# Two zero fills moved behind the last gather, weights one slot forward, and the last gate's small work moved to POOL

## The chip, the cores and the metric

The kernel runs on one core of one Trainium2 chip. The metric is the device time of one execution in microseconds; times inside a profile are counted from the start of the profiled span. A core has five engines, named here as the profile names them: PE (TensorE, with PEld for its weight loads), DVE (VectorE), ACT (ScalarE), POOL (GpSimd) and SP (SyncE, which here only issues transfers). Transfers run on 16 DMA engines.

## The reference

Sparse attention, followed by a mixture of experts with a capacity. Cut to what matters:

```python
# attention part: 4 batches x 8 heads, 768 tokens, head size 64
k_min, k_max = min / max of k over chunks of 32 keys
ub = sum_d max(q * k_min, q * k_max)          # upper bound of a chunk's scores
top_chunks = the 6 best causal chunks of each query
mask = (key's chunk in top_chunks) & causal
attn = softmax(scores masked); attn_out = attn @ v

# expert part: x = attn_out as 3072 rows of 512, 8 experts, capacity 80
logits = x @ w_gate
expert_idx = np.argmax(logits, axis=1)
gate_w = softmax(logits)[own expert]
out = np.zeros((N, D))
for e in range(E):
    tok_idx = np.where(expert_idx == e)[0]
    if len(tok_idx) > capacity:                # keep the 80 of largest gate
        tok_idx = the 80 rows with the largest gate_w
    h = np.maximum(x[tok_idx] @ w1[e], 0.0)
    out[tok_idx] = gate_w[tok_idx, None] * (h @ w2[e])
```

Every row of the output that no expert keeps is zero, so the whole output (3072 x 512 f32, 6.3 MB) is first filled with zeros, in four fills of 1.57 MB, and the kept rows are then scattered over it.

## The kernel before

All instructions are recorded through one helper, `op(engine, instruction, r=[...], w=[...])`: it notes which named pieces an instruction reads and writes, and has the engine wait for every earlier writer of what is read, and for every earlier reader and writer of what is written. `sp` and `gpd` issue transfers from SP's and POOL's queue. Each engine works in the order in which its instructions are recorded. The constants: B = 4 batches, E = 8 experts, NP = 16 pairs of heads, NT = 6 tiles of 128 tokens, CAP = 80.

The attention runs as a loop over the 16 pairs. The weights of the experts are loaded meanwhile, 1 MB at a time. Gates of batches 0 to 2 are ranked inside the loop; those of the last batch behind it. Then eight gathers fetch the kept rows, two products follow for each expert (`up`, `down`), and six blocks of 128 rows are scaled and scattered. The parts that the change and the prediction speak of:

```python
# --- writes of rows, and the gathers that read them ---
op("sp", lambda: sp.dma_start(xdst, xp[i % 2][:]), r=[f"xp{i % 2}"], w=[f"xd{i}"], dsem=...)   # in scale_rows(i)

def gather(e):
    op("gpd", lambda: gp.indirect_dma_start(
        xgv(e), None, xd, bass.IndirectOffsetOnAxis(ap=idx[:, e:e + 1], axis=0),
        bounds_check=NTOK - 1, oob_is_err=False),
        r=XD + ["idx"] + ([f"xS{e - 3}"] if e > 2 else []), w=[xgk(e)], dsem=f"d_g{e}")

# --- zero fills of the output, one for each batch: 768 rows of 2 KB ---
def fill(g, zs, zk):
    zd = bass.AP(out.tensor, out.offset + g * NT * 128 * Dm, [[Dm, 128], [128 * Dm, NT], [1, Dm]])
    op("sp", lambda: sp.dma_start(zd, zs), r=[zk], w=[f"outz{g}"], dsem=f"d_zero{g}")

# --- the loop over 16 pairs of heads (i), cut to weights and fills ---
for i in range(NP):
    scores(i, 0, 2)
    # ...
    if i == NP - 1:
        wload(E - 1, 0)                      # w1 of expert 7
    folds(i, 0, 1)
    if i == NP - 1:
        last_w2(range(4))                    # half of w2 of expert 7
    # ...
    if i == NP - 2:
        op("act", ... G[:, 0:Dm] set to 0 ...)
    # ... rank_count(bb), rows(i - 1), scale_rows(i - 1) ...
    if i == NP - 2:
        fill(3, G's zeros, "growP")
    # ...
    if 0 < i < NP - 3:
        wload((i - 1) // 2, (i - 1) % 2)     # part 0 is w1, part 1 is w2
    if i == NP - 2:
        wload(E - 2, 0)
        wload(E - 2, 1)
    if i in (0, 1, 12):
        # zeros stand in w1's buffer of expert 6 until its weights come
        fill(min(i, 2), ..., zk)

# --- the gate's digits (bf16 pieces) and masked columns, on VectorE ---
def gate_digits(b):
    op("dve", lambda: ve.tensor_copy(gsp[:, :, 0], gt6[:]), r=["gt6"], w=["gsp0"])
    op("dve", lambda: ve.tensor_tensor(gdf[:], gt6[:], gsp[:, :, 0], ALU.subtract), r=["gt6", "gsp0"], w=["gdf"])
    op("dve", lambda: ve.tensor_copy(gsp[:, :, 1], gdf[:]), r=["gdf"], w=["gsp1"])
    op("dve", lambda: ve.tensor_tensor(gsp[:, :, 2], gdf[:], gsp[:, :, 1], ALU.subtract), r=["gdf", "gsp1"], w=["gsp2"])

def last_low(jt, e):
    n = jt * 128
    o, x = Cl(jt, 0, n), G[:, S:S + n]
    if e == "dve":
        op("dve", lambda: ve.tensor_scalar(o, x, gt6[:, jt:jt + 1], None, ALU.is_lt), r=["gt6"] + gk(0, n), w=[f"L{jt}"])
    else:
        op("act", lambda: ac.activation(o, x, ACTF.Sign, bias=gt6[:, jt:jt + 1], scale=-1.0), r=["gt6"] + gk(0, n), w=[f"L{jt}"])
        op("act", lambda: ac.activation(o, o, ACTF.Relu), r=[f"L{jt}"], w=[f"L{jt}"])

# --- counting how many rows of the same expert have a larger gate ---
def last_count(order, warmth):
    for n, jt in enumerate(order):
        Cv = Cl(jt, 0, S).rearrange("p (t c i) -> p t c i", c=4, i=32)
        for c in range(4):
            op("pe", lambda: pe.matmul(MBf[c * 32:c * 32 + 32, 0:192], ohb[:, jt, :], Cv[:, :, c, :],
                                       start=(n == 0), stop=(n == NT - 1)),
               r=["ohb", f"D{jt}"] + ([f"L{jt}"] if jt else []) + ([f"U{jt}"] if jt < NT - 1 else []),
               w=["MB"], inc=(n == NT - 1 and c == 3))
        keep_warm(warmth[n])

# --- behind the loop: the last batch ---
b = B - 1
sums_last()
scale_lg(NP - 1)
gate_in(b)
gate_exp()
values(NP - 1, (0,))
sort_apply()
values(NP - 1, (1,), (0, 1), False)
gate(b)
gate_cols(b)
sort_take()
gate_digits(b)
last_row()
values(NP - 1, (1,), (1, 9), False)
last_high(0)
last_low(5, "act")
values_out(1)
last_low(4, "act")
last_low(3, "act")
last_diag(0, 1, 2, 3, 4, 5)
last_low(1, "dve")
last_high(1)
rows(NP - 1)
keep_warm(4)
last_high(4)
last_high(3)
last_low(2, "dve")
last_high(2)
scale_rows(NP - 1)
gate_gcols(b)
last_count((0, 5, 1, 4, 2, 3), (0, 0, 0, 0, 0, 6))
rank_slot(b)
rank_hot(b)
op("dve", lambda: ve.tensor_copy(dT[:, 2, :], gT[:]), r=["gT", "dT"], w=["dT"])
table(b)
merge(b)

# --- experts ---
def yv(r):                                   # four buffers for six blocks of y
    return bass.AP(EXB, 2048 + (r % 4) * 512, [[EXP, 128], [1, Dm]])

def down(r):
    # ... h @ w2 for four groups of 32 rows into OB (block 5 half into SC[0]) ...
        op("dve", lambda: ve.tensor_scalar(yv(r)[:, c0:c1], o, gR[:, r:r + 1], None, ALU.mult),
           r=[k, "gR"], w=[f"y{r % 4}"] + k0)
    op("gpd", lambda: gp.indirect_dma_start(
        out, bass.IndirectOffsetOnAxis(ap=idR[:, r:r + 1], axis=0), yv(r), None,
        bounds_check=NTOK - 1, oob_is_err=False), r=[f"y{r % 4}", "idR"] + [f"outz{g}" for g in range(B)], w=[f"out{r}"], dsem=f"d_o{r % 4}")

for e in range(3):
    gather(e)
keep_warm(4)
spread()
for e in range(4):
    t = (qT, kT)[e // 2 % 2][e % 2]
    op("dve", lambda: ve.memset(bass.AP(t, CAP // 2, [[S, 128], [HW // 2, FB], [1, (HW - CAP) // 2]]), 0.0), w=[("qT", "kT")[e // 2] + str(e % 2)])
keep_warm(12)
turn(0)
gather(3)
keep_warm(2)
up(0, lambda: turn(1, "dve"))
gather(4)
for e in range(1, E):
    if 1 < e + 1 < E:
        turn(e + 1)
        if e + 4 < E:
            gather(e + 4)
            if e + 4 == E - 1:
                last_w2(range(4, FB))
    up(e)
    if e % 4 > 0 and e != 3:
        down(e // 4 * 3 + e % 4 - 1)
    elif e == 4:
        down(2)
sy.wait_for("sp", [f"d_o{m}" for m in range(4)])
```

`last_count` takes its order of tiles and, for each, a number of warming matmuls (`keep_warm`) that keep TensorE busy and compute nothing that is used. `last_low(jt, e)` makes the comparison of tile jt with the tiles ahead of it, on VectorE or on ScalarE; it is small for a small jt.

Of the kernel before, what the change touches and what calls it, by code (L numbers as in the profile page):

```python
# [4 lines left out]
ALU = mybir.AluOpType  # L5
# [142 lines left out]
def bass_quest_chunk_select__then__topk_capacity_drop_kernel(  # L148
# [57 lines left out]
    with ExitStack() as pers:  # L206
# [17 lines left out]
        with nc.Block() as blk:  # L224

            @blk.sync
            def _body(_unused):
# [450 lines left out]
                def gate(b):  # L678
# [4 lines left out]
                    op("dve", lambda: ve.reciprocal(gt6[:], lsum[:]), r=["lsum"], w=["gt6"])  # L683
                    op("dve", lambda: ve.tensor_tensor(ohb[:, :, 0:E], oh[:], along(lmax), ALU.is_equal), r=["oh", "lmax"], w=["ohb"])

                def gate_digits(b):
                    op("dve", lambda: ve.tensor_copy(gsp[:, :, 0], gt6[:]), r=["gt6"], w=["gsp0"])
                    op("dve", lambda: ve.tensor_tensor(gdf[:], gt6[:], gsp[:, :, 0], ALU.subtract), r=["gt6", "gsp0"], w=["gdf"])
                    op("dve", lambda: ve.tensor_copy(gsp[:, :, 1], gdf[:]), r=["gdf"], w=["gsp1"])
                    op("dve", lambda: ve.tensor_tensor(gsp[:, :, 2], gdf[:], gsp[:, :, 1], ALU.subtract), r=["gdf", "gsp1"], w=["gsp2"])  # L690

                def gate_cols(b):
                    ohv = [bass.AP(ohb, 0, [[NT * 32, 128], [32, NT], [0, n], [1, E]]) for n in (2, 3)]
                    op("dve", lambda: ve.tensor_tensor(RC[:, :, 0:2, :], ohv[0], bass.AP(
                        idc, b * NT * 2, [[TOKT * 2, 128], [2, NT], [1, 2], [0, E]]), ALU.mult), r=["ohb", "idc0", "idc1"], w=["RCi"])

                def gate_gcols(b):
                    ohv = [bass.AP(ohb, 0, [[NT * 32, 128], [32, NT], [0, n], [1, E]]) for n in (2, 3)]
                    op("dve", lambda: ve.tensor_tensor(RC[:, :, 2:5, :], ohv[1], bass.AP(
                        gsp, 0, [[NT * 3, 128], [3, NT], [1, 3], [0, E]]), ALU.mult), r=["ohb", "gsp0", "gsp1", "gsp2"], w=["RCg"])  # L700

                PRED = 1.0 - 2.0 ** -24
# [209 lines left out]
                    op("act", lambda: ac.activation(bass.AP({"q": qn, "k": kn}[n][s], 0, [[NT * 2 * D, CAP], [1, 512]]), zero, ACTF.Copy, scale=0.0),  # L912
                       r=[f"{n}n{s}{g}" for g in range(4)] + ["ident_f"], w=[f"{n}n{s}0", f"{n}n{s}1"])

                def fill(g, zs, zk):
                    zd = bass.AP(out.tensor, out.offset + g * NT * 128 * Dm, [[Dm, 128], [128 * Dm, NT], [1, Dm]])
                    op("sp", lambda: sp.dma_start(zd, zs), r=[zk], w=[f"outz{g}"], dsem=f"d_zero{g}")

                def last_w2(fbs):
                    for fb in fbs:  # L920
# [9 lines left out]
                for i in range(NP):  # L930
# [7 lines left out]
                    if i:  # L938
                        sums(i - 1)
                        scale_lg(i - 1)  # L940
                    if i == NP - 1:
                        wload(E - 1, 0)
                    folds(i, 0, 1)
                    if i == NP - 1:
                        last_w2(range(4))
# [5 lines left out]
                    scores(i, 2, 4)  # L951
                    if i == 0:
                        take_r(1)
                    if i == NP - 2:
                        op("act", lambda: ac.activation(G[:, 0:Dm], bass.AP(ident_f, 0, [[128, 128], [0, Dm]]), ACTF.Copy, scale=0.0),
                           r=["ident_f"], w=["growP"])
                    if live and kk == 2:
                        rank_count(bb)
                        rank_slot(bb)
# [9 lines left out]
                        rows(i - 1)  # L969
                        scale_rows(i - 1)  # L970
                    if i == NP - 2:
                        fill(3, bass.AP(G, 0, [[2 * S, 128], [0, NT], [1, Dm]]), "growP")
                        rank_late(bb)
                    if live and kk == 0:
                        gate_exp()
# [43 lines left out]
                    if i == 11:  # L1019
                        sort_rows(False)  # L1020
                        sort_rank()
                    if 0 < i < NP - 3:
                        wload((i - 1) // 2, (i - 1) % 2)
                    if i == NP - 2:
                        wload(E - 2, 0)
                        wload(E - 2, 1)
                    if i in (0, 1, 12):
                        zk = f"w1_{E - 2}"
                        zt = bass.AP(w1s[E - 2], 0, [[DB * Fd, 128], [1, 2 * Dm]]).bitcast(F32)
                        if i == 0:  # L1030
                            op("dve", lambda: ve.memset(zt, 0.0), w=[zk])
                        fill(min(i, 2), bass.AP(w1s[E - 2], 0, [[DB * Fd, 128], [0, NT], [1, 2 * Dm]]).bitcast(F32), zk)

                b = B - 1
                sums_last()
# [2 lines left out]
                gate_exp()  # L1038
                values(NP - 1, (0,))
                sort_apply()  # L1040
                values(NP - 1, (1,), (0, 1), False)
                gate(b)
                gate_cols(b)
                sort_take()
                gate_digits(b)
                last_row()
                values(NP - 1, (1,), (1, 9), False)
                last_high(0)
                last_low(5, "act")
                values_out(1)  # L1050
                last_low(4, "act")
                last_low(3, "act")
                last_diag(0, 1, 2, 3, 4, 5)
                last_low(1, "dve")
                last_high(1)
# [4 lines left out]
                last_low(2, "dve")  # L1060
                last_high(2)
                scale_rows(NP - 1)
                gate_gcols(b)
                last_count((0, 5, 1, 4, 2, 3), (0, 0, 0, 0, 0, 6))
                rank_slot(b)
                rank_hot(b)
                op("dve", lambda: ve.tensor_copy(dT[:, 2, :], gT[:]), r=["gT", "dT"], w=["dT"])
# [59 lines left out]
                def down(r):  # L1127
                    last = r == 5
                    groups = [(r // 3 * 4 + e, sb) for e, sb in ROUNDS[r % 3]]
                    o = OB[:, r % 2 * 512:r % 2 * 512 + Dm]  # L1130
                    parts = [(o, f"O{r % 2}", 0, Dm)]
                    if last:
                        n = Dm // 2
                        parts = [(o[:, 0:n], f"O{r % 2}", 0, n), (SC[0][:, 0:n], "SC0", n, Dm)]
                    for o, k, c0, c1 in parts:
                        for fb in range(FB):
                            for g, (e, sb) in enumerate(groups):
                                op("pe", lambda: pe.matmul(o[g * 32:g * 32 + 32, :], hTv(e)[:, fb * HW + sb * 32:fb * HW + sb * 32 + 32],  # L1138
                                                           w2f(e, fb)[:, c0:c1], start=(fb == 0), stop=(fb == FB - 1)),
                                   r=[f"hT{e % 4}{fb // 4}"] + ([f"w2_{e}"] if e < E - 1 else [f"w27{f}" for f in range(FB)]), w=[k], inc=(fb == FB - 1 and g == 3))  # L1140
                        k0 = ["E2", "E3", "E4", "E5"] if r == 0 else []
                        op("dve", lambda: ve.tensor_scalar(yv(r)[:, c0:c1], o, gR[:, r:r + 1], None, ALU.mult),
                           r=[k, "gR"], w=[f"y{r % 4}"] + k0)
                    op("gpd", lambda: gp.indirect_dma_start(
                        out, bass.IndirectOffsetOnAxis(ap=idR[:, r:r + 1], axis=0), yv(r), None,
                        bounds_check=NTOK - 1, oob_is_err=False), r=[f"y{r % 4}", "idR"] + [f"outz{g}" for g in range(B)], w=[f"out{r}"], dsem=f"d_o{r % 4}")

                for e in range(3):
                    gather(e)
                keep_warm(4)  # L1150
                spread()
                for e in range(4):
# [8 lines left out]
# [3 lines that stand above are left out]
                        if e + 4 < E:  # L1164
                            gather(e + 4)
                            if e + 4 == E - 1:
                                last_w2(range(4, FB))
                    up(e)
                    if e % 4 > 0 and e != 3:
                        down(e // 4 * 3 + e % 4 - 1)  # L1170
# [38 lines left out]
```

## Time and profile before

| what | before |
|---|---|
| time, median of 3 (lowest to highest) | 290.12 us (290.0 to 290.32) |
| span of the profiled execution | 288.1 us, mean granted clock of PE 0.989 |
| busy share of PE, PEld, DVE, ACT, POOL | 95%, 59%, 74%, 51%, 79% |
| chain that ended last, by engine | PE 70%, POOL 15%, DVE 6%, DMA 4%, issue 2% |
| the loop's last value matmuls end | 245.4 us |
| first gather starts, last scatter starts | 255.05, 283.67 us |
| zero fills issued | 29.60, 41.79, 201.13, 221.31 us |
| one zero fill, issue to landing | 6.7 to 10.0 us |

A row of the chain of work gives the start, the length and what it was: an engine with the written tile and the line of the source (L1142 is line 1142), or a transfer. It is followed back from the last instruction, at each step to what released it. A row of the timeline gives start and length, engine, line, operation, written and read tiles with their shapes, and in square brackets the idle time of the engine just before with what ended it. A row of the table of stretches gives, for a stretch of time, the busy time and number of instructions of each engine, the clock that TensorE was granted (1.00 is full speed), the mean busy share of the DMA engines and the bytes moved.

The busy shares are means over two very different parts: the attention loop up to about 240 us, and the experts' part from there on, in which POOL only issues gathers and scatters.

### The profile page before, as it was taken

Reading aid. Unit: us, or ns where it says so; the run is one execution under the profiler, and the core shown is the slowest. Engines: PE = TensorE matmul, PEld = TensorE weight load, DVE = VectorE, ACT = ScalarE, POOL = GpSimd, SP = SyncE. Lnnn points to the kernel's source line nnn. Section 1 sums busy time; section 2 is a strip of 40 time slices with the busy share of each in tenths; the row PEclk is TensorE's granted clock in tenths of the full one; section 3 lists DMA queues with packets and bytes.
Section 4 is the critical chain, followed back from the end, with each engine's and each line's share of the span. In section 5 each row is a group of like instructions: output and inputs, shape, how many; then the busy total and the mean of one; then the engine's idle time right before and its main releaser. Section 6 shows DMA issues by size and latency. Waiting matters only on the chain.

```text
span 288.1 us, 8696 instructions
## 1 busy us (share of the span) xinstructions
PE 274.3 (95%) x3609; PEld 170.0 (59%) x3609; DVE 213.1 (74%) x575; ACT 147.0 (51%) x202; POOL 227.2 (79%) x295
## 2 busy tenths in 40 slices
PE   7899999999999999999999999999999999859991
PEld 7454656565656565656565656666656666428761
DVE  5897455566988989659889898898899888813341
ACT  2275656555576555555765555546756563403310
POOL 6079899998999999989999999899999970044732
PEclk9999999999999999999999999999999999998998
DMA  9999989999989999999999989995991599911361
GB/s 151 180 156 152 320 155 297 169 155 177 187 166 167 193 174 182 158 183 181 164 163 183 186 155 155 183 196 111 298 195 30 220 161 186 208 35 48 89 128 61
DMA packets 158359, 47.95 MB, mean 166 GB/s; under 512 B 142405, under 2 KB 150721, under 8 KB 158320
## 3 DMA queue, kind: packets, MB, share of 16 engines
q1 hardware_dynamic: 141664, 28.34, 50.9%
q0 software_dynamic: 13520, 18.67, 38.4%
q10 hardware_dynamic: 3136, 0.39, 0.9%
q8 instruction: 28, 0.46, 0.7%
q14 instruction: 11, 0.09, 0.1%
HBM read 53.49 MB, written 11.01 MB: 224 GB/s over the span
## 4 chain that ended last, share of the span: by engine, by line
PE 70%; POOL 15%; DVE 6%; DMA 4%; issue 2%; ACTq 1%; POOLq 0%; DVEq 0%
PE SC L509 22%; PE OB L568 19%; POOL ES L554 12%; PE SC L524 4%; PE M L595 4%; PE OB L1138 4%; PE SC L1114 4%; PE OB L641 3%; POOL EXB L545 3%; PE M L472 3%; DMA x_rows<-xp 2%; PE M L581 2%; PE MB L497 2%; DMA qn<-in_q_dram 1%; DMA qn<-x_rows,idx 1%
## 5 line engine op out<-in xcount | busy, mean ns | idle before, releaser
L531 ACT ACTIVATE EXB<-SC 128x1024 f32<-128x1024 f32 x96 | 86.2, 917 | 46.4 <-PE SC L524 45.1
L554 POOL TENSOR_TENSOR ES<-ES,EXB 128x256 f32<-128x256 f32 (+1 forms) x105 | 101.7, 980 | 4.8
L509 PE MATMUL SC<-qT,kT 64*128 64x512 f32 (+3 forms) x512 | 96.3, 466 | 0.1
L568 PE MATMUL OB<-EXB,vn 128*64 128x256 f32 (+3 forms) x704 | 72.8, 361 | 0.7 <-POOL EXB L545 0.7
L568 PEld LDWEIGHTS OB<-EXB,vn 128*64 128x64 f32 x704 | 46.9, 137 | 23.9 <-issue 9.8
L509 PEld LDWEIGHTS SC<-qT,kT 64*128 64x128 f32 x512 | 41.4, 186 | 23.0 <-issue 14.3
L554 POOL TENSOR_TENSOR ES<-EXB 128x768 f32<-128x768 f32 (+1 forms) x30 | 46.8, 1559 | 2.5
L524 PE MATMUL SC<-unsT,ind 64*128 64x128 bf16 (+5 forms) x256 | 37.7, 289 | 0.1
L576 ACT ACTIVATE oT<-OB 128x512 f32<-128x512 f32 (+1 forms) x32 | 15.6, 489 | 38.2 <-PE OB L568 38.2
L545 POOL TENSOR_SCALAR_AFFINE_SELECT EXB<-EXB 128x256 f32<-128x256 f32 x79 | 34.1, 442 | 0.0
L524 PEld LDWEIGHTS SC<-unsT,ind 64*128 64x128 bf16 x256 | 12.8, 95 | 17.9 <-issue 8.0
L439 DVE STREAM_TRANSPOSE qT<-qn 128x768 f32<-128x768 f32 x16 | 15.6, 974 | 7.2 <-PE SC L524 6.4
L586 DVE STREAM_TRANSPOSE M<-M 128x192 f32<-128x192 f32 x16 | 6.3, 394 | 19.2 <-PE M L595 18.9
L1091 POOL DMA_INDIRECT qn<-x_rows,idx x4 | 3.9, 987 | 20.8 <-DMA x_rows<-xp 19.0
L661 DVE TENSOR_TENSOR xp<-OB,rden 128x768 bf16<-128x768 f32 x16 | 15.3, 954 | 6.6 <-PE OB L641 6.3
L443 ACT ACTIVATE rq<-qT 128x768 f32<-128x768 f32 x16 | 13.5, 843 | 9.9 <-DVE qT L439 9.2
L449 DVE STREAM_TRANSPOSE kT<-kn 128x768 f32<-128x768 f32 x16 | 15.5, 966 | 1.2 <-DMA kn<-in_k_dram 1.2
L453 DVE TENSOR_REDUCE kmm<-kT 128x24 f32<-128x768 f32 x16 | 15.2, 950 | 0.5
L454 DVE TENSOR_REDUCE kmx<-kT 128x24 f32<-128x768 f32 x16 | 15.1, 942 | 0.0
L486 DVE MAX8 top<-M 128x8 f32<-128x8 f32 (+4 forms) x160 | 14.6, 164 | 0.6
L641 PE MATMUL OB<-ident_f,oT 128*128 128x128 f32 x96 | 13.9, 281 | 0.5 <-ACT oT L576 0.5
L456 POOL TENSOR_TENSOR kmm<-kmx,kmm 128x24 f32<-128x24 f32 x15 | 7.1, 471 | 9.2 <-DVE wg L907 9.2
(222 smaller groups left out, 415.6 us busy)
## 6 DMA issues: line engine op xcount, KB each, us to landing
w1s<-in_moe_w_dram POOLq DMA_DIRECT2D x8, 1024.0 KB, 9.8
w2s<-in_moe_w_dram POOLq DMA_DIRECT2D x7, 1024.0 KB, 11.2
vn<-in_v_dram SPq DMA_DIRECT2D x32, 192.0 KB, 4.8
kn<-in_k_dram SPq DMA_DIRECT2D x62, 96.0 KB, 2.7
qn<-in_q_dram SPq DMA_DIRECT2D x62, 96.0 KB, 3.1
out_dram<-w1s SPq DMA_DIRECT2D x3, 1536.0 KB, 7.8
x_rows<-xp SPq DMA_DIRECT2D x16, 192.0 KB, 6.1
out_dram<-G SPq DMA_DIRECT2D x1, 1536.0 KB, 6.9
```

The source lines that it names most:

```text
L439: op("dve", lambda: ve.transpose(qT[j][:], qn[s][:].rearrange("p a b c -> p (a b c)")), r=[f"qn{s}{g}" for g in range(4)], w=[f"qT{j}"])
L449: op("dve", lambda: ve.transpose(kT[j][:], kn[s][:].rearrange("p a b c -> p (a b c)")), r=[f"kn{s}{g}" for g in range(4)], w=[f"kT{j}"])
L453: op("dve", lambda: ve.tensor_reduce(kmm[j][:, 0, 0:NCH], kv, AX, ALU.min), r=[f"kT{j}"], w=[f"kmm{j}"])
L509: op("pe", lambda: pe.matmul(o, kT[j][pr, ts(kt)], qT[j][pr, q0:q1], start=True, stop=False), r=[f"kT{j}", f"qT{j}"], w=[f"SC{s}"], inc=False)
L524: op("pe", lambda: pe.matmul(o, ind[pr, ts(kt)], unsT[j][pr, b0 - 128:q1 - 128], start=False, stop=True), r=[f"ind{h}", f"unsT{j}"], w=[f" ...
L531: op("act", lambda: ac.activation(Ex(st, None, 0, W), src, ACTF.Exp, scale=SCALE), r=[f"SC{s}"], w=[f"E{st}"])
L545: op("gp", lambda: gp.affine_select(ad, a, pattern=[[0, 2], [1, 128]], compare_op=ALU.is_ge, fill=0.0, base=0, channel_multiplier=-1), r=[ ...
L554: op("gp", lambda: gp.tensor_tensor(o, in0, in1, ALU.add), r=[f"E{s2}", f"E{first[0]}"] if first else [f"E{s2}"] + kt, w=kt)
L568: op("pe", lambda: pe.matmul(OB[pr, q0:q1], vn[s][:, kt, h, :], ex, start=(n == 0), stop=last), r=[f"vn{s}{h}", "ES0" if st is None else f ...
L576: op("act", lambda: ac.activation(oT[:, q0:q1], OB[:, q0:q1], ACTF.Copy), r=[f"O{bk}"], w=[f"oT{bk}"])
L641: op("pe", lambda: pe.transpose(OB[:, ts(t)], oT[:, ts(t)], ident_f[:]), r=["oT0", "oT1", "ident_f"], w=[f"O{t // 4}"], inc=(t in (3, NT - ...
L661: op("dve", lambda: ve.tensor_tensor(xo, xi, rx, ALU.mult), r=["O0", "O1", "rden"], w=[f"xp{i % 2}"])
```

## The change

What it does, and what it is for:

- The zero fills of batches 2 and 3 leave the loop. They are issued by SP behind the last gather (they name its landing as something that they read), from 512 zeros that ACT writes into `ES` once the counting is over. Loop transfers thus no longer share the DMA engines with them, and the buffer of w1 of expert 6 is free of its zeros earlier.
- The weights move one slot forward: w1 of expert 6 to pass 13, w1 of expert 7 to the end of pass 14.
- Scatters 0 and 1 are recorded behind the last gather and the rest of the last w2, since every scatter must come after all fills.
- For the last batch, the gate's digits and the masked columns (`gate_digits`, `gate_cols`, `gate_gcols`) go from DVE to POOL.
- The row of gates (`last_row`, six transposes) is put ahead of the second bank's value matmuls.
- ACT makes the smallest of its three comparisons (tile 3) first, and the order of `last_count` and its warming follow: tile 4 comes last, with four warming matmuls ahead of it.

```diff
--- before.py
+++ after.py
@@ -683,20 +683,26 @@
                     op("dve", lambda: ve.reciprocal(gt6[:], lsum[:]), r=["lsum"], w=["gt6"])
                     op("dve", lambda: ve.tensor_tensor(ohb[:, :, 0:E], oh[:], along(lmax), ALU.is_equal), r=["oh", "lmax"], w=["ohb"])
 
+                def on(b):
+                    return ("gp", gp) if b == B - 1 else ("dve", ve)
+
                 def gate_digits(b):
-                    op("dve", lambda: ve.tensor_copy(gsp[:, :, 0], gt6[:]), r=["gt6"], w=["gsp0"])
-                    op("dve", lambda: ve.tensor_tensor(gdf[:], gt6[:], gsp[:, :, 0], ALU.subtract), r=["gt6", "gsp0"], w=["gdf"])
-                    op("dve", lambda: ve.tensor_copy(gsp[:, :, 1], gdf[:]), r=["gdf"], w=["gsp1"])
-                    op("dve", lambda: ve.tensor_tensor(gsp[:, :, 2], gdf[:], gsp[:, :, 1], ALU.subtract), r=["gdf", "gsp1"], w=["gsp2"])
+                    e, q = on(b)
+                    op(e, lambda: q.tensor_copy(gsp[:, :, 0], gt6[:]), r=["gt6"], w=["gsp0"])
+                    op(e, lambda: q.tensor_tensor(gdf[:], gt6[:], gsp[:, :, 0], ALU.subtract), r=["gt6", "gsp0"], w=["gdf"])
+                    op(e, lambda: q.tensor_copy(gsp[:, :, 1], gdf[:]), r=["gdf"], w=["gsp1"])
+                    op(e, lambda: q.tensor_tensor(gsp[:, :, 2], gdf[:], gsp[:, :, 1], ALU.subtract), r=["gdf", "gsp1"], w=["gsp2"])
 
                 def gate_cols(b):
+                    e, q = on(b)
                     ohv = [bass.AP(ohb, 0, [[NT * 32, 128], [32, NT], [0, n], [1, E]]) for n in (2, 3)]
-                    op("dve", lambda: ve.tensor_tensor(RC[:, :, 0:2, :], ohv[0], bass.AP(
+                    op(e, lambda: q.tensor_tensor(RC[:, :, 0:2, :], ohv[0], bass.AP(
                         idc, b * NT * 2, [[TOKT * 2, 128], [2, NT], [1, 2], [0, E]]), ALU.mult), r=["ohb", "idc0", "idc1"], w=["RCi"])
 
                 def gate_gcols(b):
+                    e, q = on(b)
                     ohv = [bass.AP(ohb, 0, [[NT * 32, 128], [32, NT], [0, n], [1, E]]) for n in (2, 3)]
-                    op("dve", lambda: ve.tensor_tensor(RC[:, :, 2:5, :], ohv[1], bass.AP(
+                    op(e, lambda: q.tensor_tensor(RC[:, :, 2:5, :], ohv[1], bass.AP(
                         gsp, 0, [[NT * 3, 128], [3, NT], [1, 3], [0, E]]), ALU.mult), r=["ohb", "gsp0", "gsp1", "gsp2"], w=["RCg"])
 
                 PRED = 1.0 - 2.0 ** -24
@@ -912,9 +918,9 @@
                     op("act", lambda: ac.activation(bass.AP({"q": qn, "k": kn}[n][s], 0, [[NT * 2 * D, CAP], [1, 512]]), zero, ACTF.Copy, scale=0.0),
                        r=[f"{n}n{s}{g}" for g in range(4)] + ["ident_f"], w=[f"{n}n{s}0", f"{n}n{s}1"])
 
-                def fill(g, zs, zk):
+                def fill(g, zs, *zk):
                     zd = bass.AP(out.tensor, out.offset + g * NT * 128 * Dm, [[Dm, 128], [128 * Dm, NT], [1, Dm]])
-                    op("sp", lambda: sp.dma_start(zd, zs), r=[zk], w=[f"outz{g}"], dsem=f"d_zero{g}")
+                    op("sp", lambda: sp.dma_start(zd, zs), r=list(zk), w=[f"outz{g}"], dsem=f"d_zero{g}")
 
                 def last_w2(fbs):
                     for fb in fbs:
@@ -938,8 +944,6 @@
                     if i:
                         sums(i - 1)
                         scale_lg(i - 1)
-                    if i == NP - 1:
-                        wload(E - 1, 0)
                     folds(i, 0, 1)
                     if i == NP - 1:
                         last_w2(range(4))
@@ -951,9 +955,6 @@
                     scores(i, 2, 4)
                     if i == 0:
                         take_r(1)
-                    if i == NP - 2:
-                        op("act", lambda: ac.activation(G[:, 0:Dm], bass.AP(ident_f, 0, [[128, 128], [0, Dm]]), ACTF.Copy, scale=0.0),
-                           r=["ident_f"], w=["growP"])
                     if live and kk == 2:
                         rank_count(bb)
                         rank_slot(bb)
@@ -969,7 +970,6 @@
                         rows(i - 1)
                         scale_rows(i - 1)
                     if i == NP - 2:
-                        fill(3, bass.AP(G, 0, [[2 * S, 128], [0, NT], [1, Dm]]), "growP")
                         rank_late(bb)
                     if live and kk == 0:
                         gate_exp()
@@ -1019,17 +1019,17 @@
                     if i == 11:
                         sort_rows(False)
                         sort_rank()
-                    if 0 < i < NP - 3:
+                    if 0 < i < NP - 2:
                         wload((i - 1) // 2, (i - 1) % 2)
                     if i == NP - 2:
-                        wload(E - 2, 0)
                         wload(E - 2, 1)
-                    if i in (0, 1, 12):
+                        wload(E - 1, 0)
+                    if i in (0, 1):
                         zk = f"w1_{E - 2}"
                         zt = bass.AP(w1s[E - 2], 0, [[DB * Fd, 128], [1, 2 * Dm]]).bitcast(F32)
                         if i == 0:
                             op("dve", lambda: ve.memset(zt, 0.0), w=[zk])
-                        fill(min(i, 2), bass.AP(w1s[E - 2], 0, [[DB * Fd, 128], [0, NT], [1, 2 * Dm]]).bitcast(F32), zk)
+                        fill(i, bass.AP(w1s[E - 2], 0, [[DB * Fd, 128], [0, NT], [1, 2 * Dm]]).bitcast(F32), zk)
 
                 b = B - 1
                 sums_last()
@@ -1038,18 +1038,18 @@
                 gate_exp()
                 values(NP - 1, (0,))
                 sort_apply()
-                values(NP - 1, (1,), (0, 1), False)
                 gate(b)
                 gate_cols(b)
+                gate_digits(b)
                 sort_take()
-                gate_digits(b)
+                gate_gcols(b)
                 last_row()
-                values(NP - 1, (1,), (1, 9), False)
+                values(NP - 1, (1,), (0, 9), False)
                 last_high(0)
+                last_low(3, "act")
                 last_low(5, "act")
                 values_out(1)
                 last_low(4, "act")
-                last_low(3, "act")
                 last_diag(0, 1, 2, 3, 4, 5)
                 last_low(1, "dve")
                 last_high(1)
@@ -1060,8 +1060,7 @@
                 last_low(2, "dve")
                 last_high(2)
                 scale_rows(NP - 1)
-                gate_gcols(b)
-                last_count((0, 5, 1, 4, 2, 3), (0, 0, 0, 0, 0, 6))
+                last_count((0, 5, 1, 3, 2, 4), (0, 0, 0, 0, 4, 0))
                 rank_slot(b)
                 rank_hot(b)
                 op("dve", lambda: ve.tensor_copy(dT[:, 2, :], gT[:]), r=["gT", "dT"], w=["dT"])
@@ -1141,12 +1140,18 @@
                         k0 = ["E2", "E3", "E4", "E5"] if r == 0 else []
                         op("dve", lambda: ve.tensor_scalar(yv(r)[:, c0:c1], o, gR[:, r:r + 1], None, ALU.mult),
                            r=[k, "gR"], w=[f"y{r % 4}"] + k0)
+                    if r > 1:
+                        scatter(r)
+
+                def scatter(r):
                     op("gpd", lambda: gp.indirect_dma_start(
                         out, bass.IndirectOffsetOnAxis(ap=idR[:, r:r + 1], axis=0), yv(r), None,
                         bounds_check=NTOK - 1, oob_is_err=False), r=[f"y{r % 4}", "idR"] + [f"outz{g}" for g in range(B)], w=[f"out{r}"], dsem=f"d_o{r % 4}")
 
                 for e in range(3):
                     gather(e)
+                op("act", lambda: ac.activation(bass.AP(ES, 0, [[2 * S, 128], [1, Dm]]), bass.AP(ident_f, 0, [[128, 128], [0, Dm]]), ACTF.Copy, scale=0.0),
+                   r=["ident_f"], w=["zero", "D0", "U0", "D1", "L1", "U1"])
                 keep_warm(4)
                 spread()
                 for e in range(4):
@@ -1164,7 +1169,11 @@
                         if e + 4 < E:
                             gather(e + 4)
                             if e + 4 == E - 1:
+                                for g in (2, 3):
+                                    fill(g, bass.AP(ES, 0, [[2 * S, 128], [0, NT], [1, Dm]]), "zero", xgk(E - 1))
                                 last_w2(range(4, FB))
+                                for r in range(2):
+                                    scatter(r)
                     up(e)
                     if e % 4 > 0 and e != 3:
                         down(e // 4 * 3 + e % 4 - 1)
```

## The prediction

> **What bounds the kernel now.** I read the chain of work that ended last first, then the timeline of the last 50 us, then the table of stretches. For the first 236 us the chain is mostly TensorE in the attention loop, and the change moves little there that the chain passes through. What it touches is the last 50 us. The chain there (start us, length us, what):
>
> ```profile
> 248.64 5.52 DMA x_rows<-xp
> ...
> 255.05 2.75 DMA qn<-x_rows,idx
> ...
> 282.39 0.50 DVE EXB L1142
> ...
> 283.44 1.20 POOLq L224
> ```
>
> The last row block of the attention output is written to memory for 5.52 us, and only then the first gather may read it. From that gather's landing (257.80) TensorE runs until the last scaling of y at 282.39; the last scatter follows. The timeline says what else the first gather waited for:
>
> ```profile
> 251.37 0.16 DVE L830 SCALAR_TENSOR_TENSOR idx<-dT 80x8 uint32<-80x8 f32 x1
> ...
> 255.05 1.05 POOL L1091 DMA_INDIRECT qn<-x_rows,idx  x1 [19.05 <-DMA x_rows<-xp]
> 256.41 0.99 POOL L1091 DMA_INDIRECT kn<-x_rows,idx  x1 [0.30 <-issue]
> 257.70 0.96 POOL L1091 DMA_INDIRECT qn<-x_rows,idx  x1 [0.30 <-issue]
> ```
>
> The indices were ready at 251.53, so at most 2.6 us of the write's 5.5 can be won before the indices are the last to come. The write is slow because of the weights: the table of stretches has the DMA share at 1.1 to 1.2 from 233 to 252 us and 0.30 at 252.5, when the last four weight transfers (w1 and w2 of expert 6, w1 of expert 7, half of w2 of expert 7) end. A write of the same 192 KB at 220.90, in a quiet stretch, took 2.9 us to land. Two more POOL lines matter for the end:
>
> ```profile
> 270.85 0.98 POOL L1091 DMA_INDIRECT kn<-x_rows,idx  x1 [0.30 <-issue]
> ...
> 283.67 0.97 POOL L1144 DMA_INDIRECT out_dram<-EXB,idR  x1 [2.16 <-DVE EXB L1142]
> ```
>
> The first is the last gather, the second the last scatter; from its start to the end of the span (288.1) are 4.4 us.
>
> **What the Trainium skill says.** "DMA: Bandwidth & Descriptors", Issuing engines are not separate DMA queues: transfers from all issuers run on the same 16 engines and interleave. The trace agrees: 5.5 us beside the weights against 2.9 alone. The same page, Anatomy of one DMA, gives a fixed cost of about 2 us plus the bytes over the bandwidth; here the scatter at 283.67 has its first bytes 1.4 us later and lands 2.7 us after its start. "TensorE: Matmul & The Clock Gate", What's actually happening: after about 3.4 us of idleness the clock is halved, and as long a busy time brings it back. The trace agrees (below). "GPSIMD Engine Reference", Performance versus the Vector engine: elementwise work on GpSimd is about half as fast as on VectorE; here POOL's 128x24 subtraction takes 0.47 us.
>
> **The change, part by part.**
>
> 1. *Weights.* Fill 2 (at 201 us) and fill 3 (at 221 us) leave the loop, so w1 of expert 6 can be issued one slot earlier, at about 216 us, where the DMA is idle from 216 to 220. What remains after 229.8 us is 1.05 MB less. At the 195 GB/s of 232 to 252 that is 5.4 us: the weights end near **247** instead of 252.5, before the last row block is issued.
>
> 2. *The write of rows.* VectorE loses four digit operations (0.2 us apart) ahead of the copy of the gate row at 243.39. That copy then waits for TensorE's transposes, which stand ahead of the first value matmuls and start at 242.12 (gate ready at 242.08) instead of 242.40; it starts at about 243.05, 0.34 earlier. The dense VectorE sequence behind it moves as a whole, so xp is done at 248.3 instead of 248.62, and the write, alone now, lands at 248.3 + 2.9 = **251.2**. It no longer decides.
>
> 3. *The indices.* The first small compare (jt 3) goes to ScalarE's front, so the output copy of the second bank moves from 245.48 to about 245.83, and with it rows (245.90 to 246.25), the four warming matmuls and the start of the counting (247.57 to 247.92). The new order has four warming matmuls *ahead of* the last count: five counts of 0.085 us, four matmuls of 0.22 us, so the last count starts at 249.2 and the transpose behind it at 249.57, where it was 248.75. The indices come 0.82 us **later**, at 252.35. POOL's digits and masks (six operations of at most about half a microsecond from 242.2) are done by 246 and hidden, as the table needs them at 250.
>
> 4. *First gather and clock.* In place of the row write the indices decide. From VectorE's result to a POOL transfer's start were 0.79 us at the last scatter: gather 0 starts at 253.15 and lands 2.75 later at **255.9**, not 257.80: 1.9 us gained. The warming matmuls now end 0.8 us before this, not 3.1, so the halved clock of this stretch (columns: busy time of PE, PEld, DVE, ACT, POOL, clock, DMA share, GB/s) goes away:
>
> ```profile
> 257.00:258.00 1.00, 0.15 (x4) 0.15 (x5) 0.00 (x0) 0.00 (x0) 0.69 (x2) 1.00 0.10 32
> 258.00:259.00 1.00, 1.00 (x9) 0.41 (x7) 0.00 (x0) 0.44 (x1) 0.66 (x1) 0.54 0.23 55
> ...
> 261.00:262.00 1.00, 1.00 (x26) 1.00 (x24) 0.49 (x1) 0.32 (x1) 0.52 (x1) 0.76 0.37 98
> 262.00:263.00 1.00, 1.00 (x31) 0.84 (x31) 0.17 (x1) 0.56 (x2) 0.54 (x2) 1.00 0.00 0
> ```
>
> That is worth up to 1.5 us, but the third gather (2.6 us behind the first) is then the limit, so I count 0.95. TensorE runs 2.85 us ahead from there. If nothing else waited, the end would be about 285.3 in the span.
>
> 5. *The fills.* They now wait for the last gather. It waits for ScalarE's copy of the fifth transpose, 268.19 before, 265.35 now; that takes 0.44, and POOL starts 0.78 after it: 266.55, landing 2.65 later, at 269.2. Only then do 2 x 1.57 MB start. The rate is that of the fill alone in the loop:
>
> ```profile
> 224.00:225.00 1.00, 1.00 (x18) 0.78 (x16) 0.97 (x4) 0.49 (x2) 1.00 (x2) 1.00 1.01 387
> 225.00:226.00 1.00, 1.00 (x16) 0.78 (x14) 0.96 (x11) 0.18 (x1) 0.92 (x2) 1.00 1.03 373
> 226.00:227.00 1.00, 1.00 (x17) 0.61 (x12) 0.52 (x3) 0.04 (x1) 1.00 (x3) 1.00 1.04 381
> ```
>
> At 383 GB/s one takes 4.1 us and both 8.2; 1.7 us pass from issue to first bytes (221.3 to 223.0), 0.7 from the last bytes to landing, and the second half of expert 7's w2, issued just before, takes about 1.0 us of the same engines. 269.25 + 1.7 + 8.2 + 1.0 + 0.7: the fills land at **280.8**.
>
> 6. *The scatters.* Every scatter waits for all fills, and scatters 0 and 1, which stood at 266.3 and 269.5, stand behind them on POOL. Scatter 0 starts at 281.6 and lands at 284.3. Blocks 0 and 4 share one y buffer, so VectorE's scaling of block 4 waits for that landing, and VectorE works in order: block 4 from 284.4 (0.75), then the second half of expert 7's activation (0.49, done 285.65), on which TensorE's last product waits. TensorE has then stood still since about 277.9, so the clock is at half: the 1.52 us from 280.77 to 282.29 become about 3.0, ending at 288.75. Half a block of scaling (0.10 + 0.50), 0.79 to POOL's start, 4.4 to the end: 288.75 + 0.6 + 0.8 + 4.4 = **294.55**, against 288.1. The sum is +6.45 us: 1.9 and 0.95 gained ahead, 9.3 lost at the end.
>
> **The rivals.**
>
> *The gain carries through.* If the fills were hidden, the time would be 290.1 - 2.85 = 287.3. For it speaks that the DMA share was only 0.1 to 0.4 from 256 to 272. Against it: 3.1 MB behind the last gather need over 8 us even at full rate, and only 11 are left before the last scatter, with five more scatters behind the wait.
>
> *Only POOL's queue binds.* Without the wait for the shared buffer and the clock, six scatters in a row, 1.3 us apart as the gathers are, start the last one at 281.6 + 6.5 = 288.1 and end at 292.5: 294.5 in time. The shared y buffer speaks against it.
>
> *Nothing gained ahead.* If the indices come later than I have them, or gathers start slower, the whole end moves with them: with no gain at step 4 the sum gives about +9.3, 299.4.
>
> **Range and chances.** 290.12 + 6.45 = 296.6. With a clock that doesn't fall, 295.1; with fills 1 us faster and the front 1 us earlier as well, 293. Scatter landings of 3.5 us, slower fills or a front without gain lead to 299. The 2% line is at 295.9, close below my centre: slower by over 2% 0.64, within 2% 0.33, faster by over 2% 0.03.
>
> **What would show it.** Right: gather 0 held by VectorE's indices near 253; clock 1.00 at 258 to 262; out_dram<-ES issued near 269 and landing near 281; a hole in TensorE of some 8 us near 278 with VectorE waiting for DMA out_dram<-EXB; six scatters in one row. Wrong: scatter 0 starting before 277 (fills faster, or earlier, than counted) leaves a time below 293; a gather 0 still held by the row write makes steps 1 and 2 false; no hole in TensorE makes the shared buffer harmless.

## The result, and the profile after

The changed kernel takes **298.61 us** (median of 4 runs, 298.38 to 298.93) against 290.06 beside it: a ratio of 1.0298, 95% interval 1.028 to 1.0316. It is slower by 8.5 us; the profiled span is 296.8 us instead of 288.1.

The chain of work that ended last, for the stretch from 240 us on in the changed kernel (start us, length us, what):

```profile
252.54 0.16 DVE idx L836
...
267.06 3.02 DMA kn<-x_rows,idx
...
270.52 12.68 DMA out_dram<-ES
...
284.11 2.75 DMA out_dram<-EXB,idR
...
286.95 0.75 DVE EXB L1141
287.70 0.41 DVE kT L1124
...
288.15 1.04 PE OB L1137 x15
289.20 1.73 PE SC L1137 x32
...
292.08 1.20 POOLq L224
```

The row write is gone from the chain. In its place stands a sequence that the kernel before did not have: the last gather (`kn<-x_rows`), then the two fills for 12.7 us, then the first scatter, then VectorE's scaling of block 4, which was waiting for that scatter, then the rest of the last product on TensorE. The two fills alone are 4% of the span, and no later row of the chain can start before they land.

The timeline of POOL shows the first gather and the first scatter with what ended their idle time:

```profile
253.69 1.08 POOL L1090 DMA_INDIRECT qn<-x_rows,idx  x1 [9.42 <-DVE idR L1081]
...
284.11 1.04 POOL L1147 DMA_INDIRECT out_dram<-EXB,idR  x1 [13.85 <-DMA out_dram<-ES]
```

The gather is now released by VectorE's small index operations (the name given is that of a neighbour of `idx`), 1.4 us earlier than the write released it before. The scatter waited 13.85 us for the fills. In the kernel before, the same scatter started at 266.29:

```profile
266.29 1.02 POOL L1144 DMA_INDIRECT out_dram<-EXB,idR  x1 [2.44 <-ACT kT L1123]
```

In the changed kernel VectorE and TensorE then stand behind this scatter:

```profile
286.95 0.75 DVE L1141 TENSOR_SCALAR EXB<-OB,gR 128x512 f32<-128x512 f32 x1 [11.69 <-DMA out_dram<-EXB,idR]
...
288.15 0.40 PE L1137 MATMUL OB<-rq,kT 128*32 128x256 bf16 x3 [9.66 <-DVE kT L1124]
```

### The profile page after: what moved, and what is told of

Read it like the earlier page. It is cut to its first block, busy times and chain, and to the rows that moved or that the text cites. A ratio compares the mean times of both kernels' runs of the same rounds, so it can differ in the third digit from the quotient of the medians.

```text
span 296.8 us, 8691 instructions
## 1 busy us (share of the span) xinstructions
PE 273.4 (92%) x3607; PEld 168.7 (57%) x3607; DVE 212.1 (71%) x569; ACT 147.0 (50%) x202; POOL 228.4 (77%) x301
## 4 chain that ended last, share of the span: by engine, by line
PE 69%; POOL 11%; DMA 8%; DVE 5%; issue 2%; ACT 1%; ACTq 1%; POOLq 0%; SPq 0%; DVEq 0%
PE SC L509 23%; PE OB L568 20%; POOL ES L554 8%; PE SC L524 5%; DMA out_dram<-ES 4%; PE OB L641 4%; PE M L595 4%; PE M L472 3%; PE M L581 2%; POOL EXB L545 2%; PE MB L497 2%; PE OB L1137 2%; DMA qn<-in_q_dram 1%; DMA kn<-x_rows,idx 1%; PE SC L1113 1%
## 5 line engine op out<-in xcount | busy, mean ns | idle before, releaser
L1147 POOL DMA_INDIRECT out_dram<-EXB,idR x6 | 6.0, 995 | 17.1 <-DMA out_dram<-ES 13.8
L1141 DVE TENSOR_SCALAR EXB<-OB,gR 128x512 f32<-128x512 f32 (+1 forms) x6 | 4.2, 707 | 18.3 <-DMA out_dram<-EXB,idR 11.7
```

## The experiments

The first four ran on a chip on which the kernel before took 289.79 us, the later ones on one on which it took 292.3 to 292.5; so times of different groups are compared by their ratio to the kernel before beside them. For the front I also use an interval inside the traces that is free of the loop's length: from the start of the gate's reciprocal on VectorE (`gt<-lsum`) to the start of the first gather.

### Fills 2 and 3 back in the loop

```diff
+ if i in (0, 1, 12): ... fill(min(i, 2), zeros in w1 of expert 6)
+ if i == NP - 2: zeros in G; fill(3, G's zeros, "growP")
- for g in (2, 3): fill(g, zeros in ES, "zero", xgk(E - 1))
  # scatters 0 and 1 recorded at their blocks again; all else as changed
```

> The changed kernel with fills 2 and 3 put back at their places in the loop and all scatters in place; weights forward, POOL's digits and the new order kept. My theory: everything lost is lost behind the fills, and the front's gain stays: the fifth transpose was 2.35 us earlier in the changed kernel than before, so the end is 2.35 us earlier than before, about 287.7 us. Rival (the fills had to leave the loop to let the weights come forward): the DMA engines are full again, the first gather waits for the row write near 255 us, and the time is about 290.

Measured: 287.68 us, ratio 0.993 (0.9908 to 0.9952). The loss is gone, and a gain stays. That the time is the forecast one to the tenth is in part luck: beside the 289.79 us of the kernel before on this chip the gain is 2.1 us, not 2.4, and a second run, in the last group below, has 0.9967, about 1 us. The first gather starts at 253.44:

```profile
253.44 1.09 POOL L1094 DMA_INDIRECT qn<-x_rows,idx  x1 [9.38 <-DVE idR L1085]
```

So the weights did not need the fills' removal: in the stretch from 224 to 232 us the DMA engines have room for fill 3, with a busy share of 0.93 in the first half and 0.20 in the second. Nor does the loop show a cost of the fills: the gate's reciprocal behind it starts at 241.88 us here and at 242.09 in the changed kernel, which has two fills fewer in the loop.

### Only the weights forward

```diff
  # kernel before, and only:
- if i == NP - 1: wload(E - 1, 0)
- if 0 < i < NP - 3: wload((i - 1) // 2, (i - 1) % 2)
+ if 0 < i < NP - 2: wload((i - 1) // 2, (i - 1) % 2)
- if i == NP - 2: wload(E - 2, 0); wload(E - 2, 1)
+ if i == NP - 2: wload(E - 2, 1); wload(E - 1, 0)
```

> The kernel before with the weights one slot forward and nothing else. My theory: the row write lands near 251 us, the indices (251.5) decide, the first gather starts at about 252.5 and the clock stays at full: some 3.5 us less than before, 286.5. Rival (the loop's fills keep the DMA engines full, so the weights end as late as before): 290.

Measured: **286.42 us** (286.31 to 286.52), ratio 0.9881 (0.9853 to 0.991): 12 us less than the changed kernel, with one of its parts. Its timeline:

```profile
251.47 0.16 DVE L830 SCALAR_TENSOR_TENSOR idx<-dT 80x8 uint32<-80x8 f32 x1
252.59 1.05 POOL L1089 DMA_INDIRECT qn<-x_rows,idx  x1 [16.69 <-DVE idR L1080]
...
280.12 0.98 POOL L1142 DMA_INDIRECT out_dram<-EXB,idR  x1 [2.16 <-DVE EXB L1140]
```

The indices come when they came before (251.47 here, 251.37 there), and the first gather follows them at once, 2.46 us earlier than before. The last scatter is 3.55 us earlier; the other 1.1 us go with TensorE's clock, which is 1.00 from 256 to 262 here and was 0.50 to 0.76 from 258 to 262 before.

### Six y buffers

```diff
- yv(r): column 2048 + (r % 4) * 512 of EXB, key y{r % 4}
+ yv(r): column 2048 + r * 512 of EXB, key y{r}
```

> The changed kernel with six y buffers, so that blocks 4 and 5 wait for no scatter. My theory: the hole in TensorE goes away, y is complete near 279 us, and then POOL's row of six scatters is the limit: the last scatter starts 1.3 us behind the fifth, at about 290.6 instead of 292.3, so 1.7 us less, 296.9. Rival 1 (the shared buffer is what costs): about 288. Rival 2 (the scatters' row is the limit anyway): no change, 298.6.

Measured: 297.07 us, ratio 1.0292 (1.0227 to 1.0358). The interval does not separate it from the changed kernel; its trace does tell the mechanism. The last block is scaled at 279.91, VectorE waits for no scatter, and POOL's scatters stand in one row:

```profile
284.34 1.04 POOL L1147 DMA_INDIRECT out_dram<-EXB,idR  x1 [14.14 <-DMA out_dram<-ES]
...
290.86 0.98 POOL L1147 DMA_INDIRECT out_dram<-EXB,idR  x1 [0.30 <-issue]
```

The last scaling ended at 280.4, about 4 us before the first scatter could go. The last starts at 290.86 instead of 292.31, and the span is 295.3 instead of 296.8. So the shared buffer is worth about 1.5 us on top of a limit that POOL's queue sets anyway. Without the fills' wait neither matters: in the kernel before POOL waited 2.16 us for VectorE ahead of the last scatter.

### One fill behind the gather instead of two

```diff
- for g in (2, 3): fill(g, ...)
+ for g in (3,): fill(g, ...)          # fill 2 in pass 12 again
```

> The changed kernel with only fill 3 behind the last gather; fill 2 back in pass 12 of the loop. My theory (the bytes of the fills set the end): 1.57 MB less at about 395 GB/s, 4.0 us less, 294.6. Rival (it is the wait for the last gather and the queue behind it, whatever the bytes): within 1 us of 298.6.

Measured: 295.08 us (293.89 to 295.84), ratio 1.0188 (1.0148 to 1.0229), against 1.0298 for both fills: 3.2 us less by the ratios. In its chain the fill takes 8.77 us, where the row of the changed kernel, which ends with the landing of both, has 12.68:

```profile
269.88 8.77 DMA out_dram<-ES
```

Taking out half of the bytes takes 4 us off the wait, so the bytes decide its length. Some 4.8 us of the 8.77 are not this fill's bytes at 395 GB/s. What is left of w2's transfers ahead of the fill, the start and the landing lie in them; no run takes them apart.

### The fills as soon as the zeros are there

```diff
- fill(g, zeros in ES, "zero", xgk(E - 1))
+ fill(g, zeros in ES, "zero")
```

> The changed kernel with fills 2 and 3 waiting only for the zeros (about 250.5 us), not for the last gather. My theory: they land near 262 us, before the first y block is ready at 263, so neither POOL nor VectorE waits for them; the first three gathers run beside them and are 1 to 1.5 us slower, so the time is about 289. Rival (behind the loop the fills cost their length wherever they stand): 295 or more.

Measured: 297.19 us, ratio 1.0223 (1.0133 to 1.0312). This expectation **missed**. The fills are issued at 250.82 and do land before the first y block, and no scatter waits for them. But the first gather has this row in the chain:

```profile
253.97 7.17 DMA qn<-x_rows,idx
```

80 rows of 1 KB take 7.17 us beside 3.1 MB of zeros, instead of 2.7. TensorE then stands for 5.0 us in front of it and starts at half clock. I had allowed 1 to 1.5 us for this; the gather lands at 261.14, when nearly all of the fills' bytes are through (the DMA share is 0.80 from 260.5 to 261 and 0.02 in the next half). Another 2.5 us of this run are two holes in TensorE for which the profile names no releaser; they stay open. They need not come from the fills: the first run without warming ahead (below), with its fills in the loop, has such a hole of 0.80 us at 261.13. The rival's number came true, but not its reason: the fills cost nothing at the scatters there.

### Warming matmuls in the hole

```diff
  up(7)
+ keep_warm(38)
  down(5)
```

> The changed kernel with 38 warming matmuls of 0.22 us ahead of the last block's product, which fill the hole in TensorE. My theory: the clock stays at full and the 2.8 us of the last product become 1.5, so 1.3 us less, 297.3. Rival (the last product waits for weights or transfers, not for the clock): no change, 298.6.

> The changed kernel with 38 warming matmuls in the hole of TensorE a second time, on a chip with less disturbance. My theory: clock 1.00 through the last product, which takes 1.5 us instead of 2.8, so 1.3 us less, 297.3. Rival 1 (transfers or weights hold the product): 298.6. Rival 2 (the matmuls added cost as much elsewhere, in waits for instructions as in the first run of this): 298.6 or more, with TensorE idle for no wait that the profile shows.

Measured: 303.71 us in the first run (299.93 to 306.87, too wide for a ratio), 301.1 in the second, ratio 1.0299 (1.0265 to 1.0332), the same as the changed kernel. Stretches of the second run (columns as in the prediction):

```profile
291.00:292.00 1.00, 0.94 (x34) 0.63 (x23) 0.01 (x1) 0.00 (x0) 0.69 (x2) 1.00 0.25 94
292.00:293.00 1.00, 0.28 (x2) 0.07 (x1) 0.48 (x1) 0.00 (x0) 0.60 (x1) 1.00 0.45 176
```

The clock is at full, and the product runs at its fast rate from 290.41 to 291.9, where the changed kernel's took from 288.15 to 290.93. But VectorE takes up the product late. The product's end is only seen at 293.6, 3.2 us behind its first matmul, where the changed kernel's took 2.8 at half clock; and the scaling of its first half starts 0.96 us behind the last matmul that the profile shows for that half, 0.05 in the changed kernel. The profile names nothing that TensorE waits for, and both runs have such a delay. So the half clock of the last product is seen, but that its removal shortens the kernel is **not** shown.

### The order of counting, and POOL's digits

All three start from the kernel with the fills in the loop.

```diff
  # no_warm_ahead: warming behind the last count, not ahead of it
- last_count((0, 5, 1, 3, 2, 4), (0, 0, 0, 0, 4, 0))
+ last_count((0, 5, 1, 3, 2, 4), (0, 0, 0, 0, 0, 4))
  # digits_dve: gate_digits, gate_cols, gate_gcols on VectorE, gate_gcols behind scale_rows
- return ("gp", gp) if b == B - 1 else ("dve", ve)
+ return ("dve", ve)
  # no_warm_digits_dve: both
```

> The kernel with the fills in the loop and weights forward, with the four warming matmuls behind the last count instead of ahead of it. My theory: the last count and the indices come 0.9 us earlier, so about 0.9 us less than the run with the fills in the loop (286.8 if that is 287.7). Rival (the count waits for ScalarE's comparison of tile 4 anyway): no change against it.

> The kernel with the fills in the loop and weights forward, with the last gate's digits and masks back on VectorE, the masked columns of the gate behind the scaling of rows as before. My theory: VectorE has 1.2 us to spare ahead of the count's transpose there, so nothing changes by more than 0.3 us against the run with the fills in the loop. Rival (VectorE's sequence sets the indices): 0.8 us more.

> The kernel with the fills in the loop and weights forward a second time, to stand beside the next two on one chip: 287.7 if before is 290.1, a ratio of 0.992.

> The same with the four warming matmuls behind the last count, a second time, on a chip with less disturbance. My theory: indices 0.9 us earlier, a ratio 0.003 below that of the run with the fills in the loop beside it. Rival (the count waits for ScalarE anyway): the same ratio.

> The kernel without the warming matmuls ahead, with the last gate's digits and masks back on VectorE. There the scaling of rows on VectorE ends as the count ends, so VectorE has nothing to spare. My theory: the copy of the gate row starts 0.35 us later, the first long comparison behind it is 0.23 us faster as POOL no longer works beside it, and the masked gate columns cost 0.2 ahead of the count's transpose: the indices come 0.3 us later, which is a ratio 0.001 higher. Rival 1 (POOL's move is worth its whole 1.2 us of VectorE's work): 1.2 us later. Rival 2 (it only slows VectorE): earlier.

| kernel | ratio to the kernel before (95% interval) | gate to first gather, us |
|---|---|---|
| before | 1 | 13.16 |
| only the weights forward | 0.9881 (0.9853 to 0.991) | 10.60 |
| changed | 1.0298 (1.028 to 1.0316) | 11.60 |
| fills in the loop | 0.993 (0.9908 to 0.9952) | 11.56 |
| the same, second run | 0.9967 (0.9938 to 0.9997) | 11.57 |
| fills in the loop, digits on VectorE | 0.9949 (0.9929 to 0.9968) | 11.58 |
| fills in the loop, no warming ahead | 0.9898 (0.9882 to 0.9914) | 10.49 |
| the same, second run | 0.9906 (0.9872 to 0.9941) | 10.49 |
| fills in the loop, no warming ahead, digits on VectorE | 0.9894 (0.9861 to 0.9927) | 10.60 |

The 11.58 comes from an execution of 294.41 us, slower than that kernel's median of 290.5. The interval of the last column repeats to 0.01 us, where the times scatter. It says: the weights forward bring 2.56 us; the four warming matmuls ahead of the last count cost 1.07; POOL's digits bring 0.11 (I had 0.3) where VectorE has nothing to spare. With the warming ahead, neither the times nor the interval (11.58 against 11.56) separate digits on POOL from digits on VectorE. So all that the change does to the front beside the weights brings 0.11 us without the warming ahead (10.49 against 10.60) and costs 0.96 with it (11.56).

Of the forecast ratios, the 0.992 for the second run with the fills in the loop **missed**, with 0.9967. The second run without warming ahead was to lie 0.003 below it and lies 0.006 below, with intervals that touch; the first pair of runs has the 0.003.

The transposes behind the count, of the changed kernel and then of the first run without the warming ahead, show where the 1.07 us lie, as an idle time of VectorE that is gone in the second:

```profile
249.90 0.40 DVE L802 STREAM_TRANSPOSE MB<-MB 128x192 f32<-128x192 f32 x1 [1.20 <-PE MB L781]
```

```profile
249.40 0.40 DVE L802 STREAM_TRANSPOSE MB<-MB 128x192 f32<-128x192 f32 x1
```

The second has no wait: the scaling of rows ends just then. (Its loop ended 0.6 us later, so the starts are to be taken against the gate, 7.81 and 6.73 us behind it.)

## Why the prediction was right, step by step

The prediction had 296.6 us, between 293.2 and 299.2, and slower by over 2% as the likeliest; measured were 298.6 and 2.98%. The mechanism was right at every step. Three terms were too small: the way to the first gather, the landing of the last one, and the end of the fills.

1. *Weights:* right. The DMA share falls from 1.17 (246 to 247 us) to 0.53 and 0.21 in the next two; I had the end near 247.
2. *The write of rows:* right. Issued at 248.72, it lands 2.2 us later, at 250.9 (251.2). It no longer decides.
3. *The indices later:* right, and a little short. They are ready at 252.70 instead of 252.35. The loop ended 0.2 us later in this execution, and from the first count to the last, with the warming between them, 1.49 us passed where I had 1.3. That the four warming matmuls ahead of the last count cause the delay is shown by the run without them.
4. *First gather and clock:* right. It starts at 253.69 (253.15): 0.99 us behind the indices, not 0.79, which with the count makes the front 0.34 us short. The clock is 1.00 from 258 to 262, as in this stretch, and ScalarE's copy of the fifth transpose starts at 265.84 (265.35), 2.35 us ahead of before; I had 2.85.

```profile
258.00:259.00 1.00, 0.71 (x21) 0.58 (x18) 0.59 (x2) 0.44 (x1) 0.91 (x1) 1.00 0.30 82
```

5. *The fills:* the mechanism right, **the size short by 1.5 us** beside what came from the front. The last gather took 3.02 us to land, not 2.65. Most of the fills' bytes moved as worked out, at about 400 GB/s from 273 to 281 us (I had 383; the three rows I took it from average 380). But I had 0.7 us from there to the landing, the value of a single fill in the loop. Stretches of the changed kernel (the first number behind the stretch is its length):

```profile
280.50:281.00 0.50, 0.00 (x0) 0.00 (x0) 0.00 (x0) 0.00 (x0) 0.00 (x0) 1.00 0.63 229
281.00:281.50 0.50, 0.00 (x0) 0.00 (x0) 0.00 (x0) 0.00 (x0) 0.00 (x0) 0.67 0.20 70
...
282.50:283.00 0.50, 0.00 (x0) 0.00 (x0) 0.00 (x0) 0.00 (x0) 0.00 (x0) 0.50 0.04 16
```

The bulk is through at 281, and a share of 0.20 down to 0.04 of the DMA engines, three of 16 falling to one or less, goes on until 283. The fills land at 283.20 (280.8). Why the end is slow stays open. The same rows show the clock fall between 281 and 281.5, some 2.7 us behind TensorE's last matmul (278.5), sooner than the 3.4 us of idleness that the prediction cites; the measurement decides.

6. *The scatters:* right. Scatter 0 starts 0.91 us behind the fills and lands 2.75 later; VectorE waited 11.7 us for it, TensorE 9.7 us for VectorE, and the rest of the last product took 2.78 us at a clock of 0.50 (I had 3.0). Only five scatters stand in one row, not the six of my list of signs: the last one waits 1.98 us more for VectorE, as my own sum had it. That the shared buffer and POOL's row are two limits, 1.5 us apart, is shown by the run with six buffers (the second rival, POOL's queue alone, stood 2.1 below the forecast). That the clock is worth 1.3 us of the time was argued, and the experiment did not show it.

The sum: 0.2 from the loop, 0.34 from the front, 0.34 from the last gather, 1.5 from the fills, 0.1 at the first scatter and 0.25 back at the product are, to a few hundredths, the 2.25 us by which the span of 296.8 exceeds the 294.55 that I had.

The first rival (the gain carries through, 287.3) is about what the change would have been without moving the fills: 287.68 in the first run of that, with less gain in the second. The third (nothing gained ahead, 299.4) is near the measured time, but not for its reason: the first gather did start 1.36 us earlier.

## What to carry to other kernels

Work that everything at the end must wait for should not be put behind a late event only because the transfer engines look idle there: count the bytes from that event on at the measured rate, then add the queue that stands behind the wait and every buffer that the queue gives back. A large transfer beside a small one that decides can cost more than its share (here 7.17 us instead of 2.7 for a gather): put it where no small transfer is on the path, here into the loop, where no cost of it shows. And when a change has several parts, the part that takes the wait away may be worth more alone: here the weights, with a ratio of 0.9881.

## What the runs showed of the hardware

- The two fills behind the last gather ended with a tail: for their last 2 us a share of 0.20 down to 0.04 of the DMA engines was busy, and the landing came behind it (281 to 283 us above; with six y buffers the share was 0.10 and 0.06 from 281 to 283 as well). The same two fills issued at 250.8 us had none: the share fell from 0.80 to 0.02 within half a microsecond at 261.
- A small gather beside 3.1 MB of fills took 7.17 us instead of 2.7.
- One of POOL's mask operations slowed VectorE beside it: the comparison of 128x640 takes 0.78 us in the changed kernel, with POOL's masks of the gate running beside it, and 0.55 with the digits on VectorE. The other runs agree: 0.78 to 0.80 with the digits on POOL, 0.55 without. That takes back 0.23 us of the VectorE time that moving them to POOL saves; the chain to the first gather of the changed kernel does not pass through this comparison.

```profile
243.83 0.78 DVE L774 TENSOR_SCALAR ES<-G,gt 128x640 bf16<-128x640 f32 x1
```

```profile
244.19 0.55 DVE L774 TENSOR_SCALAR ES<-G,gt 128x640 bf16<-128x640 f32 x1
```

The first is of the changed kernel, the second of the run without warming ahead and with digits on VectorE. "GPSIMD Engine Reference", Key points, in the Trainium skill states that GpSimd shares its SBUF interfaces with VectorE, with contention for VectorE instructions in a 2-port performance mode or with two inputs in SBUF. The slower comparison in this trace agrees with contention; in which mode it ran, no run here shows.
